# A block-sparse attention with a gated feed-forward behind it: the written-out order of all engines is replaced by another one

## The chip, the cores and the metric

One core of a Trainium2 chip. The metric is device time in microseconds (us) of one execution; lower is better.

## The reference

Inputs q, k, v of shape (4, 8, 768, 64) in float32, a list of three random blocks for each of 24 query blocks, and the weights w_in (512 x 2048), w_out (2048 x 512) and beta (2048).

```python
scores = scale * np.matmul(q, k.transpose(0, 1, 3, 2))
mask = np.abs(blk_i - blk_j) <= window        # blocks of 32, window 1
mask = mask | (blk_i == 0) | (blk_j == 0) | (blk_i == n_blocks - 1) | (blk_j == n_blocks - 1)
# and the sampled blocks of each query block
scores = np.where(mask, scores, -1000000000.0)
attn = softmax(scores);  x = (attn @ v), heads side by side: 3072 x 512
h = x @ w_in
g = h * (1.0 / (1.0 + np.exp(-beta * h)))
out = g @ w_out
```

## The kernel before

**Units.** Two heads of one batch are a pair; there are 16 pairs. A pair's 768 queries are cut into 256 and 512 (or 512 and 256), which makes 32 units, u0 to u31. For a unit, "sc" steps are the score matmuls (TensorE, 64-row halves of the array, one half for each head), "ex" the exponential (ScalarE), "mk" the mask product (VectorE; the first four units add the mask on TensorE instead), "av" the product with v, "norm" the division. The result is turned, by TensorE for the first eight units and the last pair, and by a transposing DMA otherwise, into x.

**Feed-forward tiles.** When all units of a stretch of tokens are done, its tile follows: 16 "hp" steps (x @ w_in), "th" (tanh on ScalarE), "gm" (VectorE), and then the product with w_out. The first tile takes the plain product in eight steps, 170 to 173 and 176 to 179: 170, 171, 176, 177 need rows of w_out in the first half of its chunks, 172, 173, 178, 179 those in the second half. The later tiles use a Strassen-like form ("pr" steps) with sums on VectorE ("sg") and mixed weights ("tw", steps 361 to 368).

**Loads.** q, k and v come by DMAs that SyncE issues in its own order (L504) into nine slots "st", are cast to 16 bits on VectorE or GpSimd ("cast", into "s16", or "va" for v), and are turned: by TensorE for the first pairs, by a transposing DMA on SyncE's queue from pair 4 on (L544, out `kX`, `qX`). SyncE's queue is in order: a DMA that waits holds back those behind it.

**Weights.** GpSimd issues five casting DMAs (`put`, L475 and L478): steps 73, 74, 75 bring w_in in parts of a quarter, a quarter and a half, and 76, 77 bring w_out in two halves. Step 72 (L486) is a copy of one element that waits for the load of k of pair 3 (step 54), so that 73 can't start before. Steps 234, 238 and 242 (L510) are copies of one element of w_out into a slot of pair 4's k, q and v: they hold those three loads back until the first half of w_out (234, 238) or the second (242) has landed.

**The order.** It is written out by hand or by a search in `STEPS`: `431G3` means step 431, on engine G (P TensorE, A ScalarE, D VectorE, G GpSimd, S SyncE), its result in slot 3. Each engine runs its steps in the order of this list. An entry with V (`2x192V6`) is no step: it emits matmuls on zeros into an unused bank (`emit_zeros`; four more stand ahead of the list). A cast on GpSimd also waits for the VectorE step that stands ahead of it in the list. `172P:177` is a pair of half-array steps (`in_halves`): the upper 64 rows take step 172 and the lower 64 rows step 177 at the same time; further down, `177P:172` or `177P` does the other halves. Between the two an empty instruction on GpSimd's queue (L332) waits for the first halves, and the second halves wait for it.

**Names in the profile.** Nearly all instructions are recorded in a helper at L198, so groups are told apart by their tiles: `sc<-qX,kX` sc steps, `et<-sc` ex, `et<-et,mask` mk, `sc<-va,et` av, `sc<-x,w_in_sb` hp, `sc<-g` with 128 rows the zeros, `w_mix` the tw steps, `s<-st` and `va<-st` the casts.

Of the kernel before, what the change touches and what calls it, by code (L numbers as in the profile page):

```python
# [50 lines left out]
185P3 189A3 186A6 211P0 1V2 1x256V2 182P2 1x320V3 117P2 118D3 119D0 2V3 1x448V3 109P2 197P3  # L51
120P3 212Aa 214P0 183A4 208P2 190D 110D 121D 131P3 198A0 122P6 137P7 209Ac 217P2 187D 199D 184D
200P2 123A1 132A3 124D1 143P6 133D 210D 215A9 138A2 201D2 202D4 128P1 140P3 125P0 218A2 134P4
146P2 203P5 129A1 216D 139D 213D 130D 126A3 127D 144A4 145D 135A6 147A0 141A5 220P3 221A0 238G4
234G6 235S 223P0 136D 155P4 156A3 204D8 205D 142D 158P5 159A6 224A6 164P7 206P3 161P6 162A2 148D
219D 149P2 157D 160D 222D 150A3 245P0 246A5 152P4 167P5 168A1 165A0 153A4 225D 163D 226P6 251P0
252A8 207D2 151D 248P1 249Ae 169D 229P5 227Da 166D 228D1 285P3 154D 257P0 170P4 258A1 253D 230De
231D 247D 250D 176P5:171 288P1 260P0 259D 286A2 287D 365D 366D 361D 236D0 239S 242G5 171P 254P3
172P:177 289A4 279P1 261Ad 294P0 177P 178P:173 243S 237S0 271S2 255Ab 256D 291P3 295Ac 262D
282P0 173P 280A9 296D 290D 240D5 281D 241S 179P 292A0 293D 263P7 283A7 266P3 272G2 232P1 284D  # L60
297P2 300P0 180A0 174A1 233A 402P2 367D 264Da 362D 265D3 244G1 267Dh 268D 269P1 298D1 299D0
301Dc 302D 405P3 270D 303P0 304D 403Aa 363D 364D 404D 411P1 408P2 406A6 274S4 277S6 305S5 273S3
308S8 311S7 275D4 276S 427S2 313P1 409A7 410D 412A8 413D 314A3 315D1 306G3 322P6 319P7 323A0
324D 407D 278G3 312G2 309G0 428G4 417P2 414P1 418A9 415Ae 416D 320A5 321D 331P0 316P1 317A3
332A1 318D 333D 328P4 329A0 330D 334P5 335A4 336D 325P3 326A2 435P3 436A0 438P0 337P2 340P4 419D
420P5 439Ab 444P3 441P0 338A6 327D 369D0 437D 341A3 346P3 339D 421D8 349P2 422D0 352P5 445Ac
442A2 447P0 450P3 342D 343P4 350A6 446D 347A2 443D 351D 423P2 348D 440D 355P3 448A4 449D 424Dd
425D 451A3 452D 353A3 354D 430S4 433S0 307S2 310S 181S 175S 466P3 460P0 358P2 344A4 434G0 431G3
345D 453P5 456P4 356A1 461Ad 463P0 357D 359A5 454Dh 360D 475P1 467Aa 469P3 457D3 455D1 464A3
375P5 472P0 376P 470A8 476A9 429S1 432S 485P3 491P1 372D 373D 468D 462D 458D 471D 378P4 379P  # L70
473A1 488P0 492Ac 497P1 486Ab 465D 474D 477D 481P7 478P6 489A7 494P0 498A6 500P1 495Ad 501A9
368D 377D0 380D 482D1 370D 487D 386P 597P0 598Ae 387P:383 479D2 480D3 493D 483D 499D 496D 502D
591P3 594P1 383P 604P0 617S1 620S6 426S1 459S 592A2 595Aa 607P3 608A8 605A0 384P 385A 618D1 490D
506P3 503P2 625P3 621D5 371D 623S4 638S5 388A1 626A9 610P0 611Ad 641S0 639G2 374D 504D9 505D1
# [984 lines left out]
```

## Time and profile before

| what | value |
|---|---|
| median of three runs (lowest, highest) | 265.42 us (264.58, 265.65) |
| span of the profiled execution | 265.9 us |
| TensorE, VectorE, ScalarE, GpSimd busy | 257.2, 227.7, 211.2, 35.6 us |
| granted clock of TensorE | 1.000 |
| HBM read, written | 27.27 MB, 6.29 MB |

The page gives no time for the profiled execution beside its span; the span lies 0.5 us above the median of the runs. Matmuls overlap in the records (their ends are modelled), so the busy time of TensorE says little: what counts is the spacing of their starts.

### The profile page before, as it was taken

The numbers are of one execution on the slowest core, as the hardware profiler recorded it, in microseconds if no ns is written. First come the engines' busy times: TensorE is split into PE (matmuls) and PEld (weight loads), VectorE is DVE, ScalarE is ACT, GpSimd is POOL, SyncE is SP. The second block draws the span as 40 slices with busy tenths as digits, with TensorE's granted clock in tenths as the row PEclk, the third lists the DMA queues.
The fourth block names the chain that finished last, engine by engine and source line by source line (L and its number), as shares of the span: only waits on it lengthen the run. The fifth ranks groups of instructions, "written<-read, shape, count | busy, mean of one in ns | idle before, by whom it ended". The sixth has DMA issues, their size and how long they took to land.

```text
span 265.9 us, 7061 instructions
## 1 busy us (share of the span) xinstructions
PE 257.2 (97%) x2899; PEld 168.6 (63%) x2899; DVE 227.7 (86%) x477; ACT 211.2 (79%) x284; POOL 35.6 (13%) x56
## 2 busy tenths in 40 slices
PE   8999999999998999799999999999999999999995
PEld 3575674644455875546776446766567886568884
DVE  4277999999998899599999889999879789778872
ACT  5699999889997989798976999994868876674331
POOL 4482000116020111140002103001200000000000
PEclk9999999999999999999999999999999999999999
DMA  6899994699739579625441597910504103110042
GB/s 186 285 248 232 200 215 161 138 284 258 150 59 271 138 182 271 158 67 184 127 99 55 138 257 179 237 25 0 129 11 121 22 2 120 31 42 0 5 156 79
DMA packets 50131, 36.70 MB, mean 138 GB/s; under 512 B 29732, under 2 KB 46644, under 8 KB 50100
## 3 DMA queue, kind: packets, MB, share of 16 engines
q1 hardware_dynamic: 46368, 32.06, 46.2%
q0 software_dynamic: 3664, 4.19, 9.3%
q8 instruction: 22, 0.36, 0.6%
q14 instruction: 9, 0.07, 0.1%
q10 hardware_dynamic: 68, 0.01, 0.0%
HBM read 27.27 MB, written 6.29 MB: 126 GB/s over the span
## 4 chain that ended last, share of the span: by engine, by line
PE 72%; DVE 9%; DMA 6%; ACT 5%; issue 4%; SPq 1%; POOL 1%; DVEq 0%; ACTq 0%; POOLq 0%
PE sc L198 72%; DMA qX<-s 4%; DVE et L198 4%; ACT et L198 3%; DMA st<-in_v_dram 2%; ACT t_sb L198 1%; DVE w_mix L198 1%; DVE xst L198 1%; DVE s L198 1%; SPq L504 1%; DVE g L198 1%; SPq L544 0%; DVE qX L198 0%; POOL va L198 0%; POOL s L198 0%
## 5 line engine op out<-in xcount | busy, mean ns | idle before, releaser
L198 ACT ACTIVATE et<-sc 128x1024 f16<-128x1024 f32 x144 | 139.7, 1039 | 16.6 <-PE sc L198 14.6
L198 PE MATMUL sc<-x,w_in_sb 128*128 128x512 f16 (+2 forms) x464 | 90.7, 350 | 0.2 <-DVE g L198 0.2
L198 DVE TENSOR_TENSOR et<-et,mask 128x960 f16<-128x960 f16 x132 | 83.0, 663 | 0.6 <-ACT et L198 0.6
L198 ACT ACTIVATE t_sb<-sc,beta_c_sb 128x512 f16<-128x512 f32 (+1 forms) x112 | 65.3, 640 | 22.6 <-PE sc L198 18.0
L198 DVE SCALAR_TENSOR_TENSOR g<-t_sb,sc 128x512 f16<-128x512 f16 (+1 forms) x112 | 63.8, 603 | 9.5 <-ACT t_sb L198 9.1
L198 PEld LDWEIGHTS <-w_in_sb 128*128 128x128 f16 (+1 forms) x464 | 41.7, 97 | 38.3 <-issue 5.8
L198 PEld LDWEIGHTS <-g 128*128 128x128 f16 (+1 forms) x552 | 47.9, 98 | 19.0 <-issue 8.0
L198 PE MATMUL sc<-w_out_sb,g 128*128 128x256 f16 (+3 forms) x432 | 51.8, 286 | 0.0
L198 PE MATMUL sc<-qX,kX 64*128 64x256 f16 (+1 forms) x384 | 47.8, 329 | 3.5 <-DMA qX<-s 3.1
L198 PEld LDWEIGHTS <-et 128*128 128x128 f16 x1152 | 40.4, 97 | 6.7 <-issue 2.5
L198 PE MATMUL sc<-va,et 128*128 128x65 f16 x1152 | 42.6, 193 | 0.0
L198 PEld LDWEIGHTS <-kX 64*128 64x128 f16 x384 | 17.2, 95 | 19.6 <-issue 13.7
L198 POOL CAST s<-st 128x768 f16<-128x768 f32 (+2 forms) x22 | 17.0, 784 | 82.0 <-DVE g L198 49.1
L198 PEld LDWEIGHTS <-s 128*128 128x128 f16 (+1 forms) x264 | 20.4, 98 | 5.8 <-issue 1.9
L198 PE MATMUL sc<-w_mix,s 128*128 128x256 f16 (+1 forms) x216 | 23.8, 272 | 0.1
L198 DVE TENSOR_TENSOR xst<-sc,recip 128x256 f16<-128x256 f32 x48 | 19.9, 420 | 1.0
L198 POOL CAST va<-st 128x768 f16<-128x768 f32 x13 | 11.5, 893 | 50.6 <-DVE recip L198 18.7
L198 DVE TENSOR_TENSOR osb<-osb,sc 128x512 f32<-128x512 f32 (+2 forms) x19 | 11.7, 616 | 4.8 <-PE sc L198 3.6
L198 ACT COPY osb<-sc 128x512 f32<-128x512 f32 (+3 forms) x17 | 8.8, 535 | 7.6 <-PE sc L198 6.5
L198 DVE RECIPROCAL recip<-sc 128x4 f32<-128x4 f32 x48 | 8.2, 174 | 5.5 <-PE sc L198 5.3
L198 PE MATMUL sc<-w_mix,g 128*128 128x256 f16 (+2 forms) x96 | 10.9, 264 | 0.0
L198 PE MATMUL sc<-g 128*128 128x512 f16 (+5 forms) x24 | 8.2, 426 | 1.3 <-DVE mask_blk L379 1.2
(59 smaller groups left out, 97.6 us busy)
## 6 DMA issues: line engine op xcount, KB each, us to landing
st<-in_v_dram SPq DMA_DIRECT2D x16, 384.0 KB, 5.5
out_dram<-osb SPq DMA_DIRECT2D x23, 256.0 KB, 2.3
st<-in_k_dram SPq DMA_DIRECT2D x14, 384.0 KB, 4.2
st<-in_q_dram SPq DMA_DIRECT2D x14, 384.0 KB, 5.0
w_out_sb<-in_moe_w_out_dram POOLq DMA_DIRECT2D x2, 1024.0 KB, 20.5
w_in_sb<-in_moe_w_in_dram POOLq DMA_DIRECT2D x2, 512.0 KB, 7.7
w_in_sb<-in_moe_w_in_dram POOLq DMA_DIRECT2D x1, 1024.0 KB, 13.2
st<-in_k_dram SPq DMA_DIRECT2D x4, 128.0 KB, 3.0
```

What stands on the lines that cost most here:

```text
L198: r = f(*a, **kw)
L504: nc.sync.dma_start(out=at(st)[:, :, lo * D:hi * D], in_=rows[:, :, lo * D:hi * D])
```

## The change

Only `STEPS` differs; it is three lines shorter, so all later line numbers are three lower. The 1332 steps and their work are the same. What is chosen anew is the order on every engine, the slots, the engine of some casts and copies (VectorE has 19 instead of 18 casts; 20 instead of 15 copies of the products run on ScalarE, and 24 instead of 29 on VectorE), and the half-array pairs (16 instead of 9). All 17 V entries are gone, and with them 20 matmuls on zeros; the four ahead of the list stay. The first lines, with the loads and weights, and the places that the prediction speaks of:

```diff
-0D 1V2 1x192V2 1P4 30S3 34S5 16S6 12S1 13G0 17G4 38S 44S0 31D3 39G 32P7 35D5 1x192V2 36P0 24S 20S 48S6
-3A 1x192V2 8P6 33D2 6P1 7D 25G 21G 1V2 18P3 14P7 15D0 37A 2A 9A 19A 2x192V6 89P2 90Ab 1x256V1 40P0
-1x256V1 78P1 79A4 41D 1x256V1 91P3 93P0 4P4 22P2 26P3 94Ad 45G3 49G6 46P5 27D 5D 82P0 2V3
-1x128V3 50P4 23A 92A5 80P1 58S3 54S7 28S5 72G 29G3 42S4 64S1 73G 74G 47D1 51D 83A7 81Aa 1x448V0
-100P3 101A3 102P2 103A6 104P0 105A0 52S8 53G1 59D0 68S3 55D3 75G 76G 77G 56P3 57D3 60P2 61D 84P6
-115P1 116A9 113P2 111P0 65D0 66P7 43D0 85D3 95P3 112A4 62S6 86D0 67D 87P2 88D2 191P0 194P3 114A7
-192Ae 96De 97D0 188P2 69D5 106P3 70P0 71D 63G2 10P1 98P2 11D 99D 107D0 108D4 195A1 193D 196D
...
-234G6 235S 223P0 136D 155P4 156A3 204D8 205D 142D 158P5 159A6 224A6 164P7 206P3 161P6 162A2 148D
...
-231D 247D 250D 176P5:171 288P1 260P0 259D 286A2 287D 365D 366D 361D 236D0 239S 242G5 171P 254P3
-172P:177 289A4 279P1 261Ad 294P0 177P 178P:173 243S 237S0 271S2 255Ab 256D 291P3 295Ac 262D
...
-425D 451A3 452D 353A3 354D 430S4 433S0 307S2 310S 181S 175S 466P3 460P0 358P2 344A4 434G0 431G3
...
-649P1 650A4 510P 511A4 622S 667P0 662S1 665S2 680S5 640S2 683S6 686S8 668A2 670P1 516P6 609D
...
-514A5 515D 643S 523A6 524D 526A1 520A0 672D 527D 673P3 688P0 674Ae 396P 531P4 397A 689Ab 661S3
...
+16S0 12S8 30S1 38S 34S2 24S 54S3 17G1 13G3 0D 1P0 20S 31D5 18P2 2D 3A 44S4 14P4 32P6 15D3 8P3 19D
+39D 6P1 48S1 35D0 9A 40P5 33D0 68S5 36P0 41A 58S6 78P1 25D 37D 28S7 55D4 42S0 4P0 79A7 72G 64S2
+89P3 21G 62S3 73G 91P2 7D 5A 90A0 45D1 22P0 92A1 26P3 93P3 52S8 27D 23D 82P1 49D2 94Ae 46P1 50P0
+47D1 83A2 80P3 51D 56P1 69D3 81A4 104P2 57D2 100P1 59D6 105Ab 60P1 70P0 29G1 101A3 61D 102P2 71D
+111P3 103A8 74G 65G6 43D3 113P0 115P1 114A6 95P5 63G0 116A5 66P4 84P1 75G 96Dg 67D 112Aa 191P1
+53G2 192Ac 97D0 85D0 86D4 194P2 188P3 87P0 10P3 88D1 189A9 182P0 98P2 11D 195Ad 190D 211P3 106P3
...
+202D2 135A4 164P1 145D 141A2 76G 234G0 238G4 136D 220P2 147A5 142D 148D 203P7 77G 221Ab 235S 157D
...
+225D 167P4 158P7 153A6 150A1 154D 251P1 168A2 236G5 237S3 206P5 151D 226P0 162A4 169D 159A0 163D
+252A7 229P4 242G3 240G6 227D3 228D4 160D 254P0 230D5 248P1 231D 255Aa 170P6 361D 243S 271S4 249A8
+253D 288P0 176P7:171 207D1 289A2 256D 241S 260P2 285P1 171P 261A5 365D 250D 274S1 279P0 277S7
+305S8 286A9 172P:177 366D 290D 247D 257P2 280Ac 308S5 291P1 311S6 362D 292Ad 177P 178P:173 258Ae
...
+334P5 321D 317A6 431G0 407D 435P3 335A4 337P3 309G5 327D 436A3 318D 340P1 336D 338A0 441P3 333D
+341A5 438P2 310S 432S 175S 420P0 339D 439A4 369D0 444P1 442A5 349P4 421Db 440D 422D4 342D 445A8
...
+683S4 529A4 668A9 602D2 395P 643S 513P7 663G0 512D1 399S 671Aa 519P1 664S 681G4 648D 654D 530D
...
```

More of the change, by code (lines that the diff above doesn't have):

```diff
@@ L127 @@
-1326A 1331S
+16S0 12S8 30S1 38S 34S2 24S 54S3 17G1 13G3 0D 1P0 20S 31D5 18P2 2D 3A 44S4 14P4 32P6 15D3 8P3 19D
[3 more added lines that the diff above has]
+111P3 103A8 74G 65G6 43D3 113P0 115P1 114A6 95P5 63G0 116A5 66P4 84P1 75G 96Dg 67D 112Aa 191P1
@@ new lines @@
+53G2 192Ac 97D0 85D0 86D4 194P2 188P3 87P0 10P3 88D1 189A9 182P0 98P2 11D 195Ad 190D 211P3 106P3
+193D 99D 212A0 117P4 196D 183Ae 185P3 118D1 119D3 186A2 107D2 197P0 108D1 109P5 120P3 198A3 110D
+214P3 121D 217P2 187D 199D 184D 208P1 215A6 122P0 137P1 209A1 131P7 213D 134P6 218A4 210D 216D
+155P3 128P2 123A5 200P5 129A0 124D0 132A6 130D 143P4 138A1 201Da 133D 156A0 139D 144A3 140P2 146P0
+202D2 135A4 164P1 145D 141A2 76G 234G0 238G4 136D 220P2 147A5 142D 148D 203P7 77G 221Ab 235S 157D
+239S 125P0 204Db 165A3 205D 223P2 126A1 245P1 166D 224A8 149P6 127D 222D 161P1 246A3 152P0 219D
@@ new lines @@
+275D5 267Dg 264Dc 265D0 298Dd 268D 299D1 301Dh 302D 269P0 233D 303P1 270D 405P1 408P2 304D 417P3
+409Ac 313P0 276S 367D 404D 418Ab 414P2 322P1 307S1 415A2 364D 319P7 410D 181S 314A5 416D 429S2
+328P6 406A9 325P4 315D0 413D 329A6 330D 320A1 331P2 323A4 434G3 316P0 326A2 312G2 419D 324D 332A3
+334P5 321D 317A6 431G0 407D 435P3 335A4 337P3 309G5 327D 436A3 318D 340P1 336D 338A0 441P3 333D
+341A5 438P2 310S 432S 175S 420P0 339D 439A4 369D0 444P1 442A5 349P4 421Db 440D 422D4 342D 445A8
+346P5 350A1 446D 450P3 447P0 347A2 437D 451Aa 351D 343P3 423P2 443D 424D2 348D 448Ae 352P4 344A3
@@ new lines @@
+449D 460P0 463P3 353A1 345D 358P5 461Ad 425D 452D 355P3 464A0 354D 453P2 462D 356A6 359A1 454D1
+357D 475P3 466P0 456P4 476A1 455D0 360D 472P1 467Ae 491P3 372D 375P5 473A2 469P0 457D3 458D 477D
+376P 492A8 474D 468D 378P4 470A6 465D 368D 485P3 377A1 497P1 488P0 486Ab 471D 379P 373D 489A5
+481P6 370D 498Aa 478P7 380D 490D 494P0 500P1 479D8 495A1 482D5 386P 480D3 483D 501A9 597P0 493D
+383P:387 371D 598A3 487D 499D 591P1 387P 592A4 594P0 604P3 617S5 620S4 618D3 502D 496D 595Ad 607P1
+384P 608A7 605A6 381D 385D 374D 503P0 506P1 507D3 388A0 625P1 623S6 638S2 426S0 641S1 484S 644S0
@@ new lines @@
+459S 619S3 621G4 382D 610P3 504D2 505D1 508D 626Ae 389P 593D 611A2 631P1 390P:392 599D 632Ac 652P0
+392P 628P3 653A1 649P1 629A0 646P0 659S7 662S3 509S 660D1 639D3 650A5 633D 642G5 622S 596D 393P
+640S0 665S7 606D 510P6 394D 647A8 600P7 391D 661S2 528P4 601D5 609D 627D 511A3 670P1 667P0 680S8
+683S4 529A4 668A9 602D2 395P 643S 513P7 663G0 512D1 399S 671Aa 519P1 664S 681G4 648D 654D 530D
+645G1 514A0 673P1 516P0 674Ab 522P4 517A5 630D 515D 520A0 531P3 525P2 532A1 518D 612D 521D 523A6
+396P 533D 526A3 524D 688P3 694P0 527D 651D 689A3 613P3 684G0 634P2 695A4 614D6 701P3 682S1 685S
@@ new lines @@
+397A 615D1 691P0 537P4 635D8 669D 692Ad 558D0 603S2 686S2 687G0 693D 636D0 546P5 538A0 401S 539D
+704P0 540P3 559D 702A2 547A1 675D 548D 543P4 705A6 534P2 696D 544A4 549P6 672D 535A2 541A0 555P5
+536D 550A3 624G2 545D 552P2 556A6 551D 707P0 557D 553A4 714P3 676P4 542D 708Ae 554D 655P5 715Aa
+709D 717P1 720P0 718Ac 564P6 690D 656D9 657D4 721A7 817P1 565P7:567 677D7 703D 678D3 818A9 722D
+561D 820P2 567P 814P0 821A8 808P1 815Ab 833P2 398S 400S 858S1 861S5 637S 679S 862G5 864S8 666G3
+560D 568P 658S 566A0 562D 697P0 834A0 616S 859D1 716D 572P 809A5 698Da 699D3 570D 569D 700S 836P0
@@ new lines @@
+811P2 823P1 812A1 837A4 824A3 563D 719D 573P 575P 706D 576P 819D 710P5 577A1 574D 711Db 571D 723P4
+712D2 872P0 724D3 713S 578P:581 725D4 873Ad 825D 845P2 816D 839P1 726S 581P 840A2 582P:579 846A6
+841D 866P0 891S6 894S0 822D 869P1 897S4 867Ae 579P 813D 874D 848P2 870Aa 727P01:730 849Ac 810D
+835D 583D 842P1 730P 843A7 875P2 868D 829P7 728A4 580D 826P2 731A0 729D0 827De 876A5 732D 838D
+584P 585P 828D4 850D 878P2 881P0 586A 736P2 879A9 830D8 831D 844D 733P3 737A5 847D 745P6 738D
+734A1 735D 746A6 877D 882A1 748P2 739P7 747D 905P2 895D2 749A3 899P0 924S2 832S0 927S3 860S0 590S
@@ new lines @@
+863S 925D3 851P3 928G6 892G1 893S3 926S2 900A8 854P6 906A3 750D 880D 751P2 740A2 852Dh 855De 853D2
+883D 742P5 752A0 856D 741D 902P0 743A3 760P34:763 903Ac 753D 908P3 763P 744D 909Ab 896S 587S 871D
+772P25:757 761A4 588S 911P0 764A0 762D 1013P3 929S 757P 912A0 765D 857S 910D 907D 766P3 589S 758A6
+930S1 773A1 754P1 759D 1014A2 1038S0 1041S5 774D 769P0 767A5 775D0 1044S7 884P2 770A0 768D 755A4
+1016P3 771D 887P3 1028P2 1017A4 756D 885D1 1019P0 886D1 914P3 888D4 1020A6 781P2 889D 915Ad 778D
+901D 782P 890S 779D 1029A7 784P3 916D 783A0 1058P3 913D 1049P0 785P 904D 1050A5 776D 917P5 1059A1
@@ new lines @@
+1015D 920P4 1046P3 786D 918D0 919D4 921Da 1025P0 1047A9 792P:789 922D 931D1 923S 1055P2 1026Aa
+1071P3 789P 790P:793 1051D 1018D 1072Ae 1021D 1027D 1039G1 1040S1 1056A0 1061P3 1052P0 1042G4
+865G3 793P 787D 1045D0 1062A8 1022P2 1053A3 780D 898G2 1023Ab 932P6 947P7 791D 950P0 933A1 788D
+944P1 951A6 948A3 968P4 945A0 1024D 934D1 952D 938P0 969A2 946D 962P5 949D 939A1 794A1 1060D 953P1
+963A6 1030D 954A0 959P6 1073D 970D 964D 956P7 798P 955D 940D 941P4 799P 957A6 777D 960A5 961D
+1054D 942A5 1031P5 795P 1074P0 800D 1032D7 1033D2 1063D 1034P3 804S 1043S 943D 935P6 1075Ac 958D
@@ new lines @@
+805S 1080P2 936A2 1083P0 977P7 1081Ad 937D 796P 1076D 1084A2 978A6 1035Df 1036D 971P4 797D 965P5
+1085D 972A1 979D 801P 1048D 966A6 1077P0 1057D 974P3:802 1078A4 967D 1099P3 973D 802P 1100A6 980D0
+1102P2 1082D 975A3 1096P0 1037S0 1067P6 803A 1097A7 976D 1079D 1064P7 986P2 1103A3 1068D6 983D
+1065D8 1086P0 987P3:989 1066D4 1069D 1087A8 981D 1070S 1108P3 1111P2 984D 1098D 1109A0 989P 1104D
+806S 1203P0 807S 988A0 1216P3 990P 1088D 1217A9 994P 991D 1218D 1089P6 1112A1 1204Ab 1110D 995P
+1090D0 1091D0 1105P2 1106A5 985D 1206P0 1209P3 997P 982D 1101D 996D 1210Aa 993D 1092P4 998P 1207A2
@@ new lines @@
+1093D4 1094D 1107D 1229P3 1095S 1222P2 1230A4 1219P0 1000P 1001P 992D 999D1 1113D 1223A8 1220Ac
+1211D 1208D 1117P4 1002D 1114P5 1115D9 1118Dg 1235P3 1006P:1003 1242P0 1116D4 1236Ad 1119D 1245P2
+1243Ae 1232P3 1221D 1224D 1003P 1246A1 1120P0 1205D 1121D 1233A3 1237D 1225P1 1007P 1008A 1234D
+1125P5 1126A5 1122P7 1226D7 1244D 1227D1 1248P0 1123A1 1247D 1124D0 1249A5 1250D 1231D 1004P
+1212P2 1213D9 1134P7 1214D2 1161P1 1238P2 1162A4 1135A3 1158P0 1239Db 1163D 1159A0 1128P6 1005D
+1136D 1251P1 1167P4 1252Dc 1253D3 1160D 1240D4 1155P3 1129A1 1168A2 1152P0 1215S1 1228S 1254P2
@@ new lines @@
+1146P7 1153A3 1255D 1127D 1169D 1011S 1010S 1241S 1012S 1009S 1156A0 1140P2 1154D 1137P1 1130D
+1141A5 1256P4 1257A1 1138A4 1164P0 1142D 1157D 1131P6 1139D 1165A0 1166D 1147A2 1271P3 1298P1
+1148D 1149P2 1132A6 1299A3 1258D1 1300D 1143P0 1133D 1150A1 1265P7 1295P6 1151D 1144A0 1272A5
+1145D 1296A2 1262P2 1280P5 1281A4 1263A0 1273D 1301P0 1274P1 1297D 1170D0 1176P3 1259P4 1260A1
+1275A3 1177P 1171D 1266A5 1302A6 1178A1 1264D 1179P6 1173D 1261D 1180P 1276D 1267D 1174D 1289P1
+1183D 1184P 1290A3 1182D 1277P4 1181D 1282D 1172D 1185P 1283P2 1175D 1186A 1187P 1188P 1268P5
@@ L128 @@
+1291D 1189A0 1190P 1269A4 1278A1 1284A5 1285D 1270D 1191P 1279D 1193P 1192D 1304D0 1194P 1195D
+1303D 1292P7 1286P2 1196P 1199S 1293A4 1200S 1287A3 1294D 1197P 1288D 1310P2 1198A 1307D 1308D
+1312P1 1305D 1309D 1202S 1311A1 1201S 1316P 1313D 1306D 1315D 1318P 1317A 1314D 1320P 1319A0 1322P
+1321D 1324A 1330S 1325P 1323D 1327P3 1329S 1326A 1328D 1331S
 """
```

72 lines of the change are left out of this document (2 added, 70 removed).

## The prediction

> **What bounds the kernel now.** I read the page first, then the chain of work that ended last, then the waits, then the timeline around each place where TensorE stops.
>
> ```profile
> span 265.9 us, 7061 instructions
> PE 257.2 (97%) x2899; PEld 168.6 (63%) x2899; DVE 227.7 (86%) x477; ACT 211.2 (79%) x284; POOL 35.6 (13%) x56
> ...
> 108.60 46.68 PE sc L198 x524
> 155.28 0.03 issue
> 155.30 98.33 PE sc L198 x1090
> ...
> 258.12 4.67 PE sc L198 x48
> ...
> PE sc L198 <- DMA qX<-s: 3.1, 2, 1.6
> ```
>
> TensorE is the bound, and from 108.60 us to 253.6 us the chain holds nothing else. The last row counts the waits of TensorE's matmuls for a turned q: two, 3.1 us together. A "busy" TensorE proves nothing, since matmuls overlap in the records, so I took the spacing of starts:
>
> ```profile
> 36.54 1.04 PE L198 MATMUL sc<-x,w_in_sb 128*128 128x256 f16 x8
> 37.53 0.39 PE L198 MATMUL sc<-qX,kX 64*128 64x512 f16 x2
> 37.85 1.05 PE L198 MATMUL sc<-x,w_in_sb 128*128 128x256 f16 x8
> 38.74 0.93 PE L198 MATMUL sc<-va,et 128*128 128x65 f16 x24
> ```
>
> Eight matmuls of 256 columns from 37.85 to 38.74 with no pause: 0.11 us each, about 2.4 columns a ns. From full rows to half rows the step is 37.53 - 36.54 - 0.88 = 0.11 us, back again 37.85 - 37.53 - 0.21 = 0.11 us: a change between full and half array costs about 0.1 us. With these prices I added up all matmuls of both orders. Before, from the first hp step on, the matmuls are 218.9 us and 97 changes 9.2 us (at 0.095), together 228.1 us. The first hp starts at 28.28 us (row below) and the last matmul ends at 262.8 us (258.12 + 4.67): 234.5 us. So only some 6.4 us after the start are stops, and half of that is the two waits for a turned q. What an order can gain here is small: those stops, the changes, and an earlier first hp.
>
> **The change part by part.**
>
> *Matmuls and changes.* The new order has 93 changes after its first hp and one sc step more ahead of it: 227.5 us against 228.1. That is **-0.6 us**, on the path, since TensorE sets it.
>
> *The zeros.* They stand before and between the first attention units:
>
> ```profile
> 9.36 0.42 PE L198 MATMUL sc<-shut_qk,onehot 64*128 64x256 f16 x2
> 9.57 0.42 PE L198 MATMUL sc<-qX,kX 64*128 64x256 f16 x2
> 11.02 0.27 PE L198 MATMUL sc<-qX,kX 64*128 64x256 f16 x2
> 11.13 0.27 PE L198 MATMUL sc<-shut_qk,onehot 64*128 64x256 f16 x2
> ...
> 26.10 0.78 PE L198 MATMUL sc<-g 128*128 128x512 f16 x3
> 28.28 0.94 PE L198 MATMUL sc<-x,w_in_sb 128*128 128x256 f16 x7
> ```
>
> Twenty matmuls on zeros go, 3.6 us of columns, all ahead of the first hp, where TensorE waits anyhow (ScalarE's exponentials and loads pace it). So the saving is nothing. What they may have done is seen in the first four rows: starts lie 0.21 us apart at 9.4 us and 0.11 us apart from 10.65 us on; TensorE ran at half speed until it had been kept dense from 7.0 us on. I cost their loss at nothing for the end, because the next item makes the start wait anyway; without that cover it is up to 1.8 us (half of the 3.6 us of dense work that brought the speed up). The Trainium skill (TensorE: Matmul & The Clock Gate, Part 1) says that the clock is halved until about 3.4 us of sustained work and falls back after an idle window; the trace agrees on the rise, no run here shows a fall.
>
> *Weights: the term that matters.*
>
> ```profile
> 15.03 1.66 POOL L475 DMA_DIRECT2D w_in_sb<-in_moe_w_in_dram  x2
> 15.99 1.71 SPq L504 DMA_DIRECT2D st<-in_v_dram  x1
> 17.77 0.74 POOL L475 DMA_DIRECT2D w_in_sb<-in_moe_w_in_dram  x1
> 18.50 2.05 POOL L478 DMA_DIRECT2D w_out_sb<-in_moe_w_out_dram  x2
> 24.46 0.83 POOL L198 CAST va<-st 128x768 f16<-128x768 f32 x1 [3.91 <-DMA st<-in_v_dram]
> 36.85 0.30 POOL L510 CAST st<-w_out_sb 1x1 f32<-1x1 f16 x2 [11.56 <-DMA w_out_sb<-in_moe_w_out_dram]
> 43.66 0.69 PEld L198 LDWEIGHTS <-g 64*128 64x128 f16 x8 [0.17 <-POOLq L332]
> 43.72 0.38 POOL L510 CAST st<-w_out_sb 1x1 f32<-1x1 f16 x1 [6.58 <-PE sc L198]
> ...
> GB/s 186 285 248 232 200 215 161 138 284 258 150 59 271 138 182 271 158 67 184 127 99 55 138 257 179 237 25 0 129 11 121 22 2 120 31 42 0 5 156 79
> w_out_sb<-in_moe_w_out_dram POOLq DMA_DIRECT2D x2, 1024.0 KB, 20.5
> w_in_sb<-in_moe_w_in_dram POOLq DMA_DIRECT2D x2, 512.0 KB, 7.7
> w_in_sb<-in_moe_w_in_dram POOLq DMA_DIRECT2D x1, 1024.0 KB, 13.2
> ```
>
> Before, GpSimd issues all five weight DMAs between 15.0 and 20.6 us and only then casts the last v. The first half of w_out releases steps 234 and 238 at 36.85, 18.3 us after its issue at 18.50; as the median of the two halves is their mean, 20.5, the second took 22.7 us from about 19.6: it is there at 42.3. So behind each other a half takes 42.3 - 36.9 = 5.4 us.
>
> The new order on GpSimd is 72, 21, 73, 29, 74, 65, 63, 75, 53, 76, 234, 238, **77**, 236, 242, 240, and then the empty instruction of the pair 176/171. SyncE issues the load that holds back 73 as the 7th instead of the 11th, and no load waits late for a slot, so w_in starts earlier. But 74 stands behind a v cast, 75 and 76 behind two more, and 77, the second half of w_out, behind two copies that wait for the first half to land. The two halves no longer queue behind each other.
>
> When does the second half land? The bytes ahead of it are the same as before, and at the rates of the GB/s row (slices of 6.65 us) they can't go much sooner: the 4.7 MB of first loads and a first 1.05 MB of weights take until about 24 us, the second half of w_in about 5 us more (1.05 MB at 200 to 232 GB/s), the first half of w_out 5.4, 34.4 in all. Before, it was there at 36.85; as the first slice has only 186 GB/s, room for about 0.7 MB more, I allow 3 us less, 33.8. Then 0.3 us of copies (row at 36.85), then 77 alone. What one alone takes, before does not show. At least 5.4 us; at most the 13.2 us of the w_in half that queued behind others. I take 9.5: two parts of 2.7 us each, issued 0.9 us apart, with mean 7.7 have a latency of 7.7 - 3.6 = 4.1 us, plus 5.4. The Trainium skill (DMA: Bandwidth & Descriptors, Anatomy of one DMA) gives about 2.0 us plus the bytes at 436 GB/s, an estimate of 4.4 us for 1 MB; by it the sum below would be 1.8 us lower, as this term would then cost nothing. The row that measures the queue, 5.4 us without any latency, speaks against it.
>
> So the second half lands at 33.8 + 0.3 + 9.5 = 43.6 us. Who waits: GpSimd's copy 242 (0.38 us), behind it the cast 240 (0.83 us), behind that the empty instruction, and for that TensorE with the second halves of 176/171: 43.6 + 1.2 + 0.3 = 45.1 us. Before, this place was passed at 43.66 us (PEld row), after 0.4 us more of matmuls: 43.3. **+1.8 us**; with the ends 5.4 and 13.2 it is 0 to 5.5. What the new order wins at the start (all first loads are issued by about 11 us; before, one v went out at 15.99 and was cast at 24.46) is swallowed here, so I count it as nothing.
>
> *Turned q and k.*
>
> ```profile
> qX<-s SPq DMA_TRANSPOSE x12, 3.8
> ...
> 76.15 1.21 SPq L544 DMA_TRANSPOSE qX<-s  x1
> 80.90 0.61 PE L198 MATMUL sc<-qX,kX 64*128 64x512 f16 x4 [1.62 <-DMA qX<-s]
> ...
> 100.86 0.57 SPq L504 DMA_DIRECT2D st<-in_q_dram  x1
> 101.48 0.55 SPq L504 DMA_DIRECT2D st<-in_v_dram  x1
> 102.12 1.22 SPq L544 DMA_TRANSPOSE qX<-s  x1
> 108.57 0.14 PEld L198 LDWEIGHTS <-kX 64*128 64x128 f16 x4 [1.77 <-issue]
> ```
>
> Steps 432 and 643 are the two waits, 1.62 and 1.77 us in these rows. I measured the lead of each as matmul work in the order between a cast and the reader. For 432 the cast 431 has 4.5 us before and 13.6 in the new order; for 643 it is 8.0 and 11.4, and the DMA's own place moves from 0.3 to 6.5 us ahead, against 3.8 us that a transpose takes and 6.4 that this one took behind two loads. Both waits go, nearly whole: **-3.2 us** (ends 0 and -3.4). Next late is 310: its cast's lead falls from 14.4 to 7.5 us, and 1241's from 8.6 to 4.4. In most others the lead grows. I take **+0.3 us**, 0 to 3.
>
> *The rest.* Five copies of products go from VectorE to ScalarE and as many smaller ones the other way; the two are busy 86% and 79% in the page's row, so neither is the bound: 0, and if one held TensorE up, some 0.5 us for each copy. The added empty instructions of seven more pairs lie behind one to three sc steps each, as at 43.66, where the wait was 0.17: 0. The tail has the same steps in nearly the same order: 0.
>
> Sum on the profiled span: 265.9 - 0.6 + 1.8 - 3.2 + 0.3 = 264.2. The page gives no other time for that execution, and its span lies 0.5 above the runs' median 265.42; so **263.7 us**. About 0.5% (1.3 us) is what a measurement of this kernel can tell from no change.
>
> **The rivals.**
>
> *The second half is early.* If w_out's second half is there by 41.8, the +1.8 goes and the start may count: 261.9. For it speaks the earlier 73; against it that 77 can't be issued before the first half has landed. Chance 0.20.
>
> *It is late: slower.* The release of 234 and 238 also sends out the k and q loads of pair 4, 768 KB, just ahead of 77, and the v casts ahead of 75 and 76 wait for loads that share the engines with w_in. With 13.2 us alone, from 34.5, TensorE resumes at 34.8 + 13.2 + 1.5 = 49.5: +6.2 instead of +1.8, 268.1. From a landing at 46.6 us on the result is over 0.5% slower. Middle of that case 267.5. Chance 0.20.
>
> *The waits for turned tiles only move*, to 310 or 1241, for 3 us: 266.4. For it speaks the fall of these two leads, against it the growth elsewhere. Chance 0.12.
>
> *The clock.* Without zeros TensorE may be at half speed when the hp steps start. Half speed for 3.6 us of work, 1.8 us, partly beside the wait for w_out: about 265. For it speaks the jump at 10.65, against it that with no zeros between 15.2 and 24.2 us the speed held before. The Trainium skill's clock rule (same page and section) gives this rival. Chance 0.08.
>
> **How the numbers follow.** The forecast keeps 0.40; around it 1 us either way, so 0.26 faster and 0.14 same. Early: 0.20 faster. Late: 0.20 slower. Moved waits: 0.05 same, 0.07 slower. Clock: 0.06 same, 0.02 slower. Together 0.46, 0.25, 0.29. The range goes from 1 us below the early case, 260.9, to the late case's upper part, 268.0; within it the forecast's own is 262.7 to 264.7.
>
> **What would show it.** The copy on w_out (then L507) alone near 43.6 us with a wait for w_out's DMA, and just behind it a stop of TensorE that ends with the empty instruction (then L329), 1 to 3 us long; no wait for `qX` over 0.5 us near unit 11 or 14; the first hp before 28.3 us. I am wrong if TensorE doesn't stop near 45 us, if stops for `qX` are as large as before, or if starts are 0.21 us apart after 20 us.

## The result and the profile after

The changed kernel takes **274.14 us** (273.30 to 274.66, four runs) against 265.53 us of the kernel before in the same runs: a ratio of **1.0336** [1.0291, 1.0382]. The forecast was 263.7 us, faster. The profiled execution took 273.87 us and has a span of 272.0 us, so 1.9 us lie around the span.

The page of the changed kernel: the span, the granted clock by slice, the chain by engine, and the median time of the w_out loads.

```profile
span 272.0 us, 7221 instructions
...
PEclk9999999599999999999999999999999999999999
...
PE 63%; DVE 14%; DMA 13%; issue 4%; SPq 2%; ACT 1%; POOL 1%; POOLq 0%
...
w_out_sb<-in_moe_w_out_dram POOLq DMA_DIRECT2D x2, 1024.0 KB, 12.7
```

In the eighth slice (47.6 to 54.4 us) the clock is at 0.5, which no slice of before shows. VectorE carries 14% of the chain, and not only at the start. The chain in order of time (start, duration, what):

```profile
135.70 37.17 PE sc L195 x455
...
183.77 1.20 DVE et L195
184.97 1.21 DVE g L195 x2
186.21 82.44 PE sc L195 x901
```

Before, nothing but TensorE was in it from 108.60 to 253.6 us; now VectorE's masks and gates come in between 172.87 and 186.21 too.

The timeline where the clock falls, GpSimd's and TensorE's rows (start, duration, idle before and its releaser):

```profile
36.36 0.30 POOL L507 CAST st<-w_out_sb 1x1 f32<-1x1 f16 x2 [13.01 <-DMA w_out_sb<-in_moe_w_out_dram]
36.60 0.88 POOL L475 DMA_DIRECT2D w_out_sb<-in_moe_w_out_dram  x1
43.44 0.59 PE L195 MATMUL sc<-qX,kX 64*128 64x512 f16 x4
48.30 0.17 POOL L507 CAST st<-w_out_sb 1x1 f32<-1x1 f16 x1 [6.88 <-DMA w_out_sb<-in_moe_w_out_dram]
48.46 1.26 POOL L195 CAST s<-st 128x768 f16<-128x768 f32 x1
48.54 1.89 PE L195 MATMUL sc<-w_out_sb,g 64*128 64x512 f16 x8 [4.50 <-POOLq L329]
50.65 1.91 PE L195 MATMUL sc<-w_out_sb,g 64*128 64x512 f16 x8
```

The second half of w_out (77) is issued at 36.60, behind the copies that wait for the first half, and is there at 48.2. GpSimd passes its copy at 48.30, then the pair's empty instruction, and TensorE starts again at 48.54 after 4.50 us of nothing. Then eight matmuls of 512 half-array columns take 1.89 us where e1 below has 1.04 for the same eight. The same stretch by windows (PE, PEld, DVE, ACT, POOL busy, granted clock, DMA share, GB/s):

```profile
43.70:46.00 2.30, 0.34 (x4) 0.00 (x0) 1.21 (x3) 2.26 (x3) 0.00 (x0) 1.00 1.18 174
46.00:48.50 2.50, 0.00 (x0) 0.00 (x0) 0.16 (x1) 0.00 (x0) 0.20 (x2) 0.85 0.97 142
48.50:54.50 6.00, 5.96 (x30) 2.07 (x32) 4.73 (x7) 2.07 (x3) 1.22 (x1) 0.50 0.77 186
54.50:57.00 2.50, 2.50 (x26) 1.07 (x22) 1.57 (x3) 1.65 (x2) 0.00 (x0) 0.99 1.03 361
```

The clock falls during the stop (0.85 from 46.0 to 48.5 us) and stays at 0.50 for 6 us of work: about 3.0 us lost again behind the 4.5. In steps of 0.1 us it is low from 47.7 to 54.5 us, 6.8 us in all, of which only the first 0.8 lie in the stop.

TensorE's other rows that matter, from the start and from the places where VectorE or GpSimd hold it up:

```profile
9.93 0.40 PE L195 MATMUL sc<-shut_qk,onehot 64*128 64x256 f16 x2
...
10.82 0.28 PE L195 MATMUL sc<-shut_qk,onehot 64*128 64x256 f16 x2
...
27.26 1.95 PE L195 MATMUL sc<-x,w_in_sb 128*128 128x256 f16 x16
30.65 1.05 PE L195 MATMUL sc<-x,w_in_sb 128*128 128x256 f16 x8 [1.44 <-DMA w_in_sb<-in_moe_w_in_dram]
...
106.08 1.02 PE L195 MATMUL sc<-x,w_in_sb 128*128 128x512 f16 x4 [0.57 <-DVE osb L195]
...
126.32 0.86 PE L195 MATMUL sc<-va,et 128*128 128x65 f16 x22 [0.47 <-POOL va L195]
...
135.70 0.82 PE L195 MATMUL sc<-qX,kX 64*128 64x512 f16 x6 [0.50 <-DVE xst L195]
...
186.21 1.02 PE L195 MATMUL sc<-x,w_in_sb 128*128 128x512 f16 x4 [0.78 <-DVE g L195]
```

The step to full speed comes where it came before, without the zeros: starts lie 0.21 us apart up to 10.14 us and 0.11 us from 10.82 on, against 10.65 before; from 27.26 on sixteen matmuls of 256 columns take 1.95 us. Hp starts at 27.26 but waits 1.44 us for the third weight load, which now stands behind casts of v. Four stops of 0.47 to 0.78 us, 2.3 together, are where the order before has none.

### The profile page after: what moved, and what is told of

It reads as the page before. It is cut to its first block, busy times and chain, and to the rows that moved or that the text cites. A ratio compares the mean times of both kernels' runs of the same rounds, so it can differ in the third digit from the quotient of the medians.

```text
span 272.0 us, 7221 instructions
## 1 busy us (share of the span) xinstructions
PE 256.2 (94%) x2979; PEld 168.2 (62%) x2979; DVE 231.7 (85%) x478; ACT 212.4 (78%) x284; POOL 38.9 (14%) x55
## 3 DMA queue, kind: packets, MB, share of 16 engines
HBM read 27.27 MB, written 6.29 MB: 123 GB/s over the span
## 4 chain that ended last, share of the span: by engine, by line
PE 63%; DVE 14%; DMA 13%; issue 4%; SPq 2%; ACT 1%; POOL 1%; POOLq 0%
PE sc L195 63%; DMA w_out_sb<-in_moe_w_out_dram 5%; DVE et L195 5%; DMA st<-in_k_dram 4%; DVE g L195 4%; DMA st<-in_v_dram 4%; DVE s L195 2%; SPq L501 2%; ACT et L195 1%; DVE osb L195 1%; DVE xst L195 1%; DVE va L195 1%; POOL s L195 0%; DVE recip L195 0%; ACT t_sb L195 0%
## 5 line engine op out<-in xcount | busy, mean ns | idle before, releaser
L195 DVE TENSOR_TENSOR et<-et,mask 128x960 f16<-128x960 f16 x132 | 85.6, 680 | 4.5 <-ACT et L195 4.4
L195 PEld LDWEIGHTS <-g 128*128 128x128 f16 (+1 forms) x612 | 46.5, 98 | 22.6 <-issue 7.3
L195 PE MATMUL sc<-w_out_sb,g 128*128 128x256 f16 (+3 forms) x496 | 55.3, 295 | 4.5 <-POOLq L329 4.5
L195 PE MATMUL sc<-qX,kX 64*128 64x512 f16 (+1 forms) x384 | 49.8, 333 | 1.0 <-DVE xst L195 0.5
L195 POOL CAST s<-st 128x768 f16<-128x768 f32 (+2 forms) x21 | 19.4, 930 | 103.3 <-PE sc L195 46.4
L195 PE MATMUL sc<-w_mix,s 128*128 128x256 f16 (+1 forms) x224 | 22.0, 271 | 0.0
L195 ACT COPY osb<-sc 128x512 f32<-128x512 f32 (+3 forms) x22 | 11.8, 536 | 10.2 <-PE sc L195 8.9
L195 POOL CAST va<-st 128x768 f16<-128x768 f32 x13 | 12.7, 993 | 16.9 <-PE sc L195 7.4
L195 DVE TENSOR_TENSOR osb<-osb,sc 128x512 f32<-128x512 f32 (+2 forms) x19 | 11.6, 615 | 4.0 <-PE sc L195 1.8
L195 PE MATMUL sc<-w_mix,g 128*128 128x256 f16 (+3 forms) x112 | 13.2, 264 | 0.0
L195 DVE CAST s<-st 128x768 f16<-128x768 f32 (+2 forms) x16 | 8.5, 544 | 4.9 <-DMA st<-in_k_dram 4.9
```

Of the source, the lines that this page charges most:

```text
L195: r = f(*a, **kw)
```

## The experiments

Twelve kernels were run, four in each of three sets. The kernel before had 264.59, 264.06 and 265.46 us in them. Each ratio is to the kernel before in the same set.

**e1: the second half behind the first.** One entry of the changed list is moved.

```diff
-141A2 76G 234G0 238G4 ... 203P7 77G 221Ab
+141A2 76G 77G 234G0 238G4 ... 203P7 221Ab
```

> Theory 1, the release order: in the changed kernel step 77 (second half of w_out) stands behind 234 and 238, which wait for the first half; it lands at 47.9 us, TensorE stops for 4.7 us behind GpSimd's empty instruction and then runs about 6 us at half clock (3 us lost). With 77 right behind 76 both go: 264 to 266.5 us. Theory 2, the new order as a whole is worse and the stop only hides that something else is late (VectorE, turned tiles): less than half comes back, 270 us or more.

Measured: 267.91 us (267.45 to 268.56), ratio 1.0136 [1.0092, 1.0179], between the two theories. Some 5 to 6 us come back (0.0200 of the time by the ratios, 6.2 us by the medians). TensorE's rows:

```profile
30.35 0.83 PE L195 MATMUL sc<-x,w_in_sb 128*128 128x256 f16 x6 [1.17 <-DMA w_in_sb<-in_moe_w_in_dram]
...
44.31 1.04 PE L195 MATMUL sc<-w_out_sb,g 64*128 64x512 f16 x8 [0.57 <-POOLq L329]
...
51.53 0.39 PE L195 MATMUL sc<-qX,kX 64*128 64x512 f16 x2 [1.65 <-DMA qX<-s]
```

The stop of 4.50 is 0.57 us, and the clock does not fall. What was hidden behind it comes up: 1.65 us for a turned q at 51.5. So 77's place is the larger part of the loss, not all of it.

**e2: the clock held up through the stop.** Twenty-one matmuls on zeros stand in the stop of the changed kernel.

```diff
-260P2 285P1 171P
+260P2 285P1 21x512V0 171P
```

> The changed kernel with 21 matmuls on zeros (4.5 us at full speed) in the place of the stop. Theory 1 with the clock as a cost of its own: the stop stays, the granted clock stays at 1.00 from 46 to 55 us, and about 3 us come back: 271. Rival, the half clock lies beside waits of other engines and costs nothing: 274.

Measured: 272.31 us (269.05 to 272.62), ratio 1.0259 [1.0179, 1.0339]: by the medians 1.8 us less than the changed kernel, not 3. TensorE's timeline, and the windows behind the stop:

```profile
43.93 4.69 PE L195 MATMUL sc<-g 128*128 128x512 f16 x21
50.23 1.04 PE L195 MATMUL sc<-w_out_sb,g 64*128 64x512 f16 x8 [1.61 <-POOLq L329]
```

```profile
50.20:56.00 5.80, 5.57 (x50) 2.35 (x50) 5.77 (x9) 3.99 (x5) 1.21 (x1) 1.00 0.75 182
```

The clock stays at 1.00 and the eight matmuls are back to 1.04 us; but in this execution 77 took 13.4 us instead of 11.6, so TensorE starts again at 50.23 instead of 48.54. The half clock behind the stop is caused by the stop. What it is worth the times alone don't settle, as the intervals of the two ratios overlap; the two profiled executions do: from TensorE's new start to the end of the span it is 223.5 us in the changed kernel and 220.6 us here, 2.9 us less.

**e3: the kernel before with the one step late.**

```diff
-75G 76G 77G 56P3 ... 234G6 235S
+75G 76G 56P3 ... 234G6 77G 235S
```

> The kernel before with one step moved: 77 behind 238 and 234 on GpSimd. Theory 1: the half lands 10 to 11 us after its issue at 37, so at 47.5 to 48; TensorE needs it at 46.2 us for step 172: it stops 1.5 to 2.5 us, and with lost clock after that 267 to 269. Rival, covered by other work: 265.5.

Measured: 272.52 us (271.42 to 274.33), ratio 1.0315 [1.0254, 1.0375]. A single step of 1332 makes nearly the whole loss, more than either theory had:

```profile
50.40 1.89 PE L198 MATMUL sc<-w_out_sb,g 64*128 64x512 f16 x8 [6.28 <-DMA w_out_sb<-in_moe_w_out_dram]
```

Here no empty instruction is between; TensorE waits for the DMA itself, 6.28 us, and then runs at half clock. It does so for a shorter time than in the changed kernel:

```profile
52.00:54.00 2.00, 2.00 (x14) 0.90 (x12) 1.35 (x3) 0.82 (x1) 0.00 (x0) 0.63 0.69 203
54.00:56.00 2.00, 2.00 (x22) 0.95 (x18) 1.76 (x4) 1.77 (x3) 0.00 (x0) 1.00 0.77 152
```

In steps of 0.1 us the clock is low from 46.7 to 53.4 us, again 6.8 us, but 3.7 of them lie in the stop. The stop and half of the 3.0 us of work that are left make 7.8 us, which is the loss measured (7.9 us by the medians).

**e4: is it GpSimd's queue or the data?** The copies that wait for the second half go behind the pairs.

```diff
-229P4 242G3 240G6 ... 361D 243S 271S4 ... 173P 262D
+229P4 240G6 ... 361D 271S4 ... 173P 242G3 243S 262D
```

> The changed kernel with the copy 242 and its load moved behind the three half-array pairs, so that no empty instruction of a pair stands behind the wait for w_out; 77 stays late. Theory 1 by the data: step 172 needs the second half itself, about 1.1 us of matmuls later, so the stop shrinks by 1 us only: 273. Rival, the coupling through GpSimd's queue is the cause: the stop goes, 266 to 268.

Measured: 272.21 us (269.56 to 273.69), ratio 1.0263 [1.0188, 1.0338]. The profile is of the shortest of the four executions (269.56 us). The empty instruction no longer waits, and TensorE stops one step later:

```profile
47.38 1.04 PE L195 MATMUL sc<-w_out_sb,g 64*128 64x512 f16 x8 [2.61 <-DMA w_out_sb<-in_moe_w_out_dram]
```

It is the data that is late; in the changed kernel the queue only chooses where that is felt. The clock falls here too, at 48.6 us, when TensorE has been at work again for 1.2 us, and is back at 52.0.

**e5 and e6: the two lists cut and joined.** e5 has the old order up to step 174 and the new one behind it, e6 the new order up to step 180 and the old one behind it; a buffer number is changed only where a slot is still held at the seam.

```diff
 e5: (before) ... 180A0 174A1 | (after, steps not yet done) ...
 e6: (after)  ... 179P ... 180A1 | (before, steps not yet done) ...
```

> The order of the kernel before up to and with step 174 (286 steps: the first attention units, all weight loads, the first products with w_out), then the changed order for the other 1046 steps; 12 buffer numbers differ from the changed kernel's where a slot is still held at the seam. Theory 'start': all of the loss lies in the first 55 us, and the changed order behind it is as good as the old one or gains the two waits for turned q: 261.5 to 264.8 us. Theory 'rest': the stops of 0.73, 0.54, 0.57 and 0.94 us that the changed kernel shows at 105, 125, 135 and 185 us cost what is left in e1_second_half_first (3.3 us over the kernel before): 266 to 268 us.

> The opposite: the changed order up to and with step 180 (287 steps), then the order of the kernel before for the other 1045; 2 buffer numbers differ. Theory 'start': 273 to 275 us, with the stop of 4.7 us near 43.7 and half clock behind it. Theory 'rest': 270 to 271.5 us, as the stops at 105 to 185 us are gone.

Measured: e5 269.31 us (268.48 to 272.10), ratio 1.0220 [1.0156, 1.0285]; e6 277.70 us (276.40 to 278.39), ratio 1.0528 [1.0500, 1.0557]. Both miss both theories, because the seam makes stops of its own. In e5 there are two just behind it, and the clock falls with them; e6 keeps the stop at 43 us, now of 5.41 us, and has another at 105 us, again with the clock. First e5's rows, then e6's and its windows:

```profile
53.97 0.39 PE L196 MATMUL sc<-qX,kX 64*128 64x512 f16 x2 [1.17 <-ACT et L196]
56.13 1.01 PE L196 MATMUL sc<-identity,xst 128*128 128x128 f16 x8 [1.77 <-DVE xst L196]
```

```profile
49.05 1.46 PE L194 MATMUL sc<-w_out_sb,g 64*128 64x512 f16 x6 [5.41 <-POOLq L328]
...
107.03 0.58 PE L194 MATMUL sc<-x,w_in_sb 64*128 64x512 f16 x2 [1.75 <-DMA x<-xst]
```

```profile
105.30:107.00 1.70, 0.00 (x0) 0.00 (x0) 1.67 (x5) 0.40 (x1) 0.00 (x0) 1.00 1.22 40
107.00:108.50 1.50, 1.47 (x10) 0.76 (x11) 1.50 (x3) 0.42 (x1) 0.00 (x0) 0.53 0.90 257
108.50:110.00 1.50, 1.50 (x12) 0.82 (x10) 0.67 (x2) 0.86 (x2) 0.00 (x0) 0.50 1.00 318
110.00:111.00 1.00, 1.00 (x9) 0.35 (x6) 0.00 (x0) 1.00 (x2) 0.00 (x0) 0.74 0.82 281
```

As a split of the loss these two are inconclusive: e5 is 5.3 us and e6 13.6 us above the kernel before, which adds to far more than the change's own 8.6.

**e7: all weight loads back to back.** On top of e1, the third w_in load and both halves of w_out go ahead of the casts of v.

```diff
-... 74G 65G6 ... 75G 96Dg ... 141A2 76G 234G0 ... 203P7 77G 221Ab
+... 74G 75G 76G 77G 65G6 ... 96Dg ... 141A2 234G0 ... 203P7 221Ab
```

> The changed kernel with the third and fourth weight load and both halves of w_out issued right behind the second one on GpSimd, ahead of the casts of v that stood between them. In e1_second_half_first there were left at the start: a wait of 1.3 us at 28.9 us for the third weight load, 0.7 at 43.4 for the pair's empty instruction, 1.8 at 48.9 for a turned q. Theory 'start': the first two go, 265.3 to 266.4 us. Theory 'bandwidth': loads of v and weights share the engines, so what the weights gain the casts of v lose, and the waits only move to the first products with v near 20 us: 267.5 to 268.5 us.

Measured: 265.95 us (265.41 to 267.06), ratio 1.0082 [1.0055, 1.0110]. The wait for w_in and the one for the pair are gone from TensorE's rows; one for the turned q stays:

```profile
29.55 2.21 PE L195 MATMUL sc<-x,w_in_sb 128*128 128x256 f16 x18
...
51.03 0.39 PE L195 MATMUL sc<-qX,kX 64*128 64x512 f16 x2 [0.44 <-DMA qX<-s]
```

In its profile the first hp comes at 29.55 instead of 27.27 in e1, so in part the waits did move, as the second theory had it; by the time the first theory fits. Against e1 that is 0.0054 of the time less, which the two intervals only just set apart from nothing.

**e8: the kernel before, profiled again.** The same list, nothing edited.

```diff
 (no difference to the kernel before)
```

> The kernel before, profiled once more. If the two waits for a turned q (1.62 us at 80.9, 1.77 at 108.6) belong to its order, they are there again, and the span is 265 to 266 us. If they belong to the one execution that was profiled (its span of 265.9 is 3 us above those of the timed runs, 261.4 to 263.9), one or both are absent, with a span of 262 to 263.5 us; then the 3.2 us that were credited for them were not in the median time.

Measured: 265.14 us, span 263.2 us. From the page and TensorE's timeline:

```profile
span 263.2 us, 7061 instructions
```

```profile
26.65 1.49 PE L198 MATMUL sc<-x,w_in_sb 128*128 128x256 f16 x12
...
78.61 0.61 PE L198 MATMUL sc<-qX,kX 64*128 64x512 f16 x4 [1.04 <-ACT et L198]
...
105.82 0.39 PE L198 MATMUL sc<-qX,kX 64*128 64x256 f16 x4 [1.03 <-DVE g L198]
```

Both waits are there again, but smaller: 1.04 and 1.03 us in place of the 1.62 and 1.52 of the same rows in the first profile (the prediction's 1.77 is the row of the weight load). Their ends are put down to ScalarE and VectorE here; that it is still the turned q that is late is shown by e9, which moves only that. The first hp is at 26.65, not 28.28. The execution whose profile the prediction rested on was 2.7 us longer than this one, by 1.6 us at the start and 1.1 in these waits.

**e9: only the turned q earlier, in the kernel before.**

```diff
-344A4 434G0 431G3 345D
+344A4 431G3 434G0 345D
-680S5 640S2 683S6 686S8 ... 515D 643S 523A6
+680S5 640S2 643S 683S6 686S8 ... 515D 523A6
```

(So 643 passes two loads, 683 and 686; 680 stands ahead of it as before, other than the expectation says.)

> The kernel before with two moves only: on GpSimd the q cast 431 ahead of the v cast 434 that waits some 9 us for its slot, and on SyncE the turned q 643 ahead of the loads 680, 683 and 686. Theory 'the waits were real and go': the stops of 1.1 us at 77 and 1.2 us at 104 us of e8_before_again vanish with nothing late behind them: 2.0 to 2.4 us less than the kernel before, about 261.8 us against 264.1. Theory 'they only move': the next late tile or load takes their place, within 0.5 us of the kernel before.

Measured: **263.74 us** (262.20 to 264.98), ratio **0.9951** [0.9920, 0.9982], the lowest of this study. The rows at the two places show no idle time before them:

```profile
78.35 0.70 PE L195 MATMUL sc<-qX,kX 64*128 64x512 f16 x4
...
104.26 0.67 PE L195 MATMUL sc<-qX,kX 64*128 64x256 f16 x8
```

The gain, 1.3 us (0.5 to 2.1 by the interval), lies between the two theories; it is at the low side of the two waits' 2.1 us.

**e10: the kernel before without its twenty matmuls on zeros.**

```diff
-0D 1V2 1x192V2 1P4 ... 35D5 1x192V2 36P0 ... 119D0 2V3 1x448V3 109P2
+0D 1P4 ... 35D5 36P0 ... 119D0 109P2
```

> The kernel before without its twenty matmuls on zeros, which are not part of the result. Theory 'nothing hangs on them' (the prediction's step): within 0.5 us of the kernel before, as loads and ScalarE pace TensorE there. Theory 'they hold the clock': half speed somewhere before 28 us, 1 to 3 us slower. Theory 'they stand in the way': up to 1.5 us faster, as some of their 3.6 us lie on the path to the first product with w_in at 28.3 us.

Measured: 264.95 us (262.62 to 267.80), ratio 0.9995 [0.9961, 1.0028]: no difference that the interval, some 1 us to each side, could show. The prediction's step on the zeros holds.

**e11: the second half alone on the DMA engines.**

```diff
-77G 221Ab 235S 157D 239S ... 236G5 237S3 ... 242G3 240G6 ... 243S ... 241S
+77G 221Ab 157D ... 242G3 ... 243S 235S 239S 236G5 237S3 240G6 241S
```

> The changed kernel with the k and q loads of pair 4 (235, 239), their casts and their turned tiles put behind the second half of w_out, so that for some 10 us its DMA has the engines to itself. In the changed kernel it was issued at 36.6 and landed at 47.9: 11.3 us. Theory 'company': the two loads of 384 KB cost it 2 us or more, and it takes 8.5 to 9.5 us, the 9.5 that the prediction took. Theory 'its own pace': a half takes over 10.5 us however alone. The time as a whole is no test, as TensorE will want the late q and k: 273 to 280 us.

Measured, in one run: 275.91 us. The issues of the window 36 to 37.5 us, of the changed kernel and then of e11 (KB each, us from issue to landing):

```profile
w_out_sb<-in_moe_w_out_dram POOLq DMA_DIRECT2D x1, 1024.0 KB, 11.6
st<-in_k_dram SPq DMA_DIRECT2D x1, 384.0 KB, 3.9
st<-in_q_dram SPq DMA_DIRECT2D x1, 384.0 KB, 6.6
```

```profile
w_out_sb<-in_moe_w_out_dram POOLq DMA_DIRECT2D x1, 1024.0 KB, 9.3
```

Alone it takes 9.3 us, with the two loads beside it 11.6. Company costs 2.3 us; the first theory is borne out. In the changed kernel a turned k, issued at 41.45, runs beside it too, but in e3 only the two loads do, and there 77 took 12.4 us; in e4 it took 11.7. The time of e11 as a whole says nothing of this: the data is there at 45.9 us, but the empty instruction now stands behind the casts of the late k and q, and TensorE starts again only at 52.27.

**e12: back to back, and three moves on VectorE.** On top of e7:

```diff
-606D 510P6 394D            -716D 572P 809A5 698Da 699D3    -1024D 934D1 952D 938P0
+394D 606D 510P6            +698Da 699D3 716D 572P 809A5    +952D 1024D 934D1 938P0
```

(606 and 394, 716 and 698, 1024 and 952 have other steps between them, which stay.)

> e7_weights_back_to_back with three more moves on VectorE, for the stops left in it at 99, 128 and 178 us (0.32, 0.57, 0.93 us): the copy 394 ahead of the mask step 606, the division 698/699 ahead of the mask step 716, the gate product 952 ahead of the mask step 1024 and of 934. Theory 'rest': the three stops are what keeps it behind the kernel before, and it comes to 264.0 to 264.4 us, equal to the kernel before. Theory 'start': they are not, and it stays at 265.5 to 266 us.

Measured: 264.76 us (263.76 to 266.03), ratio 0.9998 [0.9965, 1.0032], against 1.0082 of e7. The three late waits of TensorE that e7's profile has (0.16, 0.50 and 0.77 us, 1.4 together) are gone. The chain of its page, by engine:

```profile
PE 81%; DMA 8%; ACT 5%; DVE 3%; SPq 1%; issue 1%; POOL 0%; ACTq 0%; POOLq 0%
```

VectorE's part is 3% where the changed kernel had 14%. With seven entries moved in all, the changed order is equal to the kernel before, as the first theory had it, though 264.76 us lies a little over its range.

## Why the prediction was wrong

**The weights, the step that failed.** The place was right: the copy alone on w_out, a stop of TensorE behind it that ends with the empty instruction, first named for 43.6 to 45.1 us. The size was not: +1.8 us was forecast, and 4.50 us of stop and some 3 us of half clock came. Three terms of its sum were off:
- The first half was to land at 33.8 us, 3 us earlier than before; its copies ran at 36.36 against 36.85. The new start brought it hardly forward (in e8, the second profile of before, they ran at 36.53), and 77 went out 2.5 us later than assumed.
- Its own 9.5 us was right for a transfer alone (9.3 in e11). But 77 is released together with the k and q loads of pair 4 by the same copies, and with them it took 11.6, so the sum had this term 2.1 us too small. The prediction saw these loads and priced them only in a rival. By the Trainium skill (DMA: Bandwidth & Descriptors, Anatomy of one DMA) 4.4 us had been an estimate for this transfer; the 9.3 us measured alone decide against it.
- In the other direction, 0.83 us for the cast 240 should not have been in the sum: TensorE starts at 48.54, while that cast runs from 48.46 for 1.26 us.

**The clock.** The prediction looked for half clock only at the start, for want of zeros. That cost nothing (e10, and the rows at 9.93 and 10.82 us). But a stop of the 1.8 us that it forecast itself can already bring the clock down (1.75 us in e6), and no step asked what follows the stop. So 3.0 us were put at nothing. The Trainium skill (TensorE: Matmul & The Clock Gate, Part 1) says that the clock falls after an idle window of about 3.4 us; the prediction cited that rule as one that no run showed. The changed kernel shows a fall in its stop of 4.50 us; e6 shows one with a stop of only 1.75 us, which is less than that figure, and there the measurement decides.

The rival *It is late: slower* had the right mechanism and threshold (a landing behind 46.6 us; it was 48.2), but at 267.5 us it lacked the clock, and it had a chance of 0.20.

**Turned q and k.** The two waits go in the changed kernel, as forecast, and e9 shows that this is a gain: 1.3 us. The credit of 3.2 was too large, since it came from the one profiled execution, which was 2.7 us longer than the second; there the waits are 2.1 us. That the span of 265.9 us lay so near the runs' median of 265.42 hid this: in e8 and in the changed kernel the time is 1.9 us over the span, so that execution took some 267.8 us, an estimate, and was 2.4 us longer than the median.

**The rest.** It was put at 0, on the ground that VectorE at 86% is not the bound. The chain, with VectorE in it up to 186 us, and the four stops of 2.3 us together contradict that; e12 takes three such stops, 1.4 us in e7's rows, out of e7 by order alone and gains 1.2 us by the medians and 0.0084 of the time, 2.2 us, by the ratios of their two sets. Mean use hid what one late instruction does.

**Matmuls, changes, zeros.** Nothing contradicts -0.6 and 0; only the zeros were tried by themselves. The start, counted as nothing, was no gain either: the first hp is at 27.26 us, against 28.28 and 26.65 in the two profiles of before.

From the span of e8 to that of the changed kernel, 263.2 to 272.0: first hp +0.6, third weight load +1.4, stop +4.5, half clock +3.0, late stops +2.3, turned q -2.1, matmuls and changes -0.6: 9.1 of 8.8 us. The runs bear the large terms out one by one: 77's place (e1, 0.0200 of the time against the changed kernel's ratio), the rest of the weights (e7, 0.0054), VectorE's order (e12, 0.0084); all three are differences between sets: the first is good to a third of its size, the last to a half, and the middle one is only just clear of nothing. What stays open is the turned q that waits near 51 us in e1, e7 and e12; and why e5 and e6 stop at their seams was not followed further.

## What to carry to other kernels

When a load is moved behind a wait, its new landing is the landing of what it waits for, plus its own time, plus the time of everything that the same release sets off; take that company into the forecast itself, not only into a rival. A stop of TensorE of about 2 us or more can cost more than its length: add the half clock behind it, 1.5 to 3 us in these runs. And profile the kernel before twice, before a gain is read off waits of 1 to 2 us: here they differed by a third between two executions.

## What the runs showed of the hardware

- The granted clock fell to 0.50 with stops of TensorE of 4.50 us (changed kernel), 6.28 us (e3), 5.41 and 1.75 us (e6), 2.61 us (e4), 8.19 us (e11), and 1.17 and 1.77 us close together (e5); it held through 1.62 us (the first profile), 1.65 us (e1) and 1.61 us (e2). The fall came between 1.7 us (e5) and 5.1 us (e11) after TensorE had last stopped, in e4 only when it had been at work again for 1.2 us, so the length of a stop alone does not tell when it comes.
- Once low, the clock stayed low for one of two lengths, read in steps of 0.1 us: 6.8 us (changed kernel, e3, the first fall of e6, e11) or 3.4 us (e4, e5, the second fall of e6). TensorE was busy in 6.0 us of the 6.8 in the changed kernel and in 3.0 us of them in e3, so a low stretch of one length cost 3.0 us in one and 1.5 us in the other.
- At the start the granted clock reads 1.00 in both kernels, though starts lie 0.21 us apart up to about 10 us; there the spacing of starts tells more.
- A 1 MB weight load on GpSimd's queue took 9.3 us with nothing issued beside it (e11, one run) and 11.6 to 13.4 us beside the k and q loads of 384 KB that the same release sends out (changed kernel, e2, e3, e4, e6); in the changed kernel these took 3.9 and 6.6 us.
- The start is not the same from run to run: the first hp step of the same order stood at 28.28 and 26.65 us in two executions.
- An empty instruction on GpSimd does not wait for the end of the cast ahead of it: TensorE was released at 48.54 us, 0.08 us after that cast began, and again 0.07 to 0.08 us after it in e2, e6 and e11 (spans on GpSimd are rough).
